# Seven half-depth products for the last four weight blocks of a first fp32 layer

## The chip, the cores and the metric

One core of one Trainium2 chip. The metric is device time of one execution in microseconds (us), the median of several runs.

## The reference

A retention layer (a decayed linear attention; 2 batches, 8 heads, 768 positions, head size 64) feeds two feed-forward layers, each with its own weights and curve. All arithmetic is in fp32; the weights and q, k, v are drawn at random.

```python
state = gamma * state + k_t (x) v_t          # for each batch and head
y_t   = q_t @ state / sqrt(64)
x = y as [1536 tokens, 512]                  # n_tokens = 2 * 768
h = x @ w_in;  g = softplus(h);    x = g @ w_out        # layer one, d_ff = 2048
h = x @ w_in2; g = s * relu(h)**2 + b;  out = g @ w_out2   # layer two
```

## The kernel before

**Number format.** TensorE multiplies in fp32r. Every fp32 operand is split into a high part (a copy rounded to fp32r, made by ScalarE) and a low part (operand minus high part, made by GpSimd or VectorE), and a product is three matmuls: high x high, high x low, low x high. The names end in `h` and `l`: `xh`/`xl` (the layer's input), `gh`/`gl` (the curve's output), `wh`/`wl` (weights).

**Tiles.** Tokens form three tiles (`j` = 0, 1, 2) of 512. Each layer has 16 blocks of 128 hidden units; the blocks are numbered 0 to 15 in layer one and 16 to 31 in layer two. For a block and a tile, the *first product* (12 matmuls of 128x128 by 128x512, one PSUM bank) gives h; the curve and the split give `gh`, `gl`; the *second product* (12 matmuls, `acc_mm` or `acc_2`) adds to four PSUM banks (`acc`) which hold one tile's 512 output columns. After some blocks those four banks are added to `xa[j]` in SBUF (`take_out`, `take_2`) and are used for the next tile. There is one set of these four banks. Beside them there are the banks `h`, `y`, `third` for first products and `word` for the weights' bits.

**Two ways of going through a layer.** In *steps* (`steps`, `step`), four blocks go through the three tiles, one block and one tile at a time: 12 steps for a group of four blocks, each with one first product (`h_mm`, 12 matmuls) and the second product of three steps earlier. In *pairs*, two blocks are taken together. `plain` makes all of their first products as 12 matmuls each (`all_of`), six of them. `second` uses seven half-depth products (`six`, 6 matmuls each, Strassen's scheme in Winograd's form) for tiles 0 and 1 of the two blocks, where plain products would take eight times six; tile 2 is done plainly in layer one. Each product of `second` is followed by a second product of earlier blocks. The seven products need four sums of weights (`sums_w`: four 128x256 sums on GpSimd; `split_sums`: their high parts on ScalarE, low parts on GpSimd) and four sums of x (`sum_x`, `parts_x`: t1 to t4), and their results are joined by copies on ScalarE (`kept`: p1, p5, u2) and adds on VectorE (`joined`).

**Order of layer one before.** Blocks 0 to 3 in steps, blocks 4 and 5 plain, blocks 6 to 11 as three pairs by `second(0, 3)` to `second(0, 5)`, and blocks 12 to 15 in twelve steps again. `take_out` after those steps adds the sums to `xa` on VectorE and splits the result into `xh` (ScalarE) and `xl` (GpSimd) for tiles 0 and 1; for tile 2, `sum_last` and `parts_last` do it, reading from PSUM. Layer two starts with `plain(1, 0)` (blocks 16 and 17), whose loop index k = 0 to 5 is called plain product 0 to 5 here, in the order tile 0 block 16, tile 0 block 17, tile 1 block 16 and so on. Then come `second(1, 1)` (blocks 18 and 19; during it the sums `sum_z` are made on VectorE for a finer scheme of tile 2 in the later pairs) and `second(1, 2)` to `second(1, 7)`.

**Weights.** They come as 64-bit words and are made into fp32 by `split_w`, in four pieces spread over the products by `part`, `go_first`, `go_last`, `end_part` and `go`: two VectorE operations (L291, L293) with a ScalarE copy (L296) into a buffer `wm` of which there are two, a VectorE operation (L301), and the split (ScalarE, GpSimd). The list `halves` gives their order, and also when `sums_w` (written `(w, 2)`) and `split_sums` (`(w, 3)`) run. The copy L296 of a weight must wait until all that read its `wm` buffer are done, `sums_w` among them.

**What sets the order.** Nothing is scheduled by a planner: each engine works through its own queue in the order in which the program issues to it, and waits in order. Within a product of `plain` in layer two the issue order is: the product, the curve (three ScalarE operations: relu L567, square L592, scale L593), the split of g (ScalarE, GpSimd), the pieces of weights left over, the second product, further weight pieces, `sum_x`, `parts_x`.

Of the kernel before, what the change touches and what calls it, by code (L numbers as in the profile page):

```python
# [13 lines left out]
P = 128  # L14
# [13 lines left out]
NG = NF // FG  # L28
# [14 lines left out]
P0, P1 = FG // 2, PAIRS - FG // 2  # L43
# [6 lines left out]
def tile_retention_mlps(ctx: ExitStack, tc: tile.TileContext, head, w1, w2, sb, out):  # L50
# [282 lines left out]

    steps = [(0, g, j, f4) for g in range(NG) for j in range(NTILE) for f4 in range(FG)]

# [46 lines left out]
    def act_3(s):  # L382
        gg_t[s] = next_g() if s >= GS else [gp.tile([P, TT], F32R, tag=t, name=t) for t in ("gh", "gl")]
# [24 lines left out]
    def take_out(s, cc):  # L408
        la, g, j, f4 = steps[s]
        ps, dst = acc_t[la, g, j][cc], xa[j][:, cc, :]  # L410
        if g == 0:
            nc.scalar.activation(dst, ps, AF.Copy)
        else:
            nc.vector.tensor_tensor(out=dst, in0=ps, in1=dst, op=ALU.add)
        if g == NG - 1:
            split(xh[j][:, cc, :], xl[j][:, cc, :], dst, nc.scalar, nc.gpsimd)


    def sum_last(banks):

        la, g, j, _ = steps[NS - 1]
        for cc in banks:
            t = acc_t[la, g, j][cc]
            nc.vector.tensor_tensor(out=t, in0=t, in1=xa[j][:, cc], op=ALU.add)

    def parts_last():
        la, g, j, _ = steps[NS - 1]
        ps = acc_t[la, g, j]
        for cc in range(KC):
            nc.scalar.activation(xh[j][:, cc], ps[cc], AF.Copy)  # L430
        for cc in range(KC):
            nc.vector.tensor_tensor(out=xl[j][:, cc], in0=ps[cc], in1=xh[j][:, cc].bitcast(F32), op=ALU.subtract)
# [228 lines left out]
    for p in range(P0, P1):  # L661
        halves += pair(0, p)
    at[0, P1] = len(halves)
    for w in (2 * P1, 2 * P1 + 2):
        halves += [(w, 0), (w + 1, 0)]
    halves += [(w, 1) for w in range(2 * P1, NF)]
# [96 lines left out]
    with tc.manual_schedule():  # L763
# [198 lines left out]
        def plain(la, p, left, sums, parts):  # L962
# [5 lines left out]
            for k, (j, half) in enumerate((j, half) for j in range(NTILE) for half in range(2)):  # L968
# [3 lines left out]
                if la and k == 2:  # L972
                    end_part()
                    accs[k]()
# [7 lines left out]
                if not la or k != 2:  # L982
                    accs[k]()
# [6 lines left out]
        def second(la, p):  # L990
# [3 lines left out]
            halved = la and p >= HALVED  # L994
            base -= halved
# [83 lines left out]
            if before:  # L1079
                parts_z(2)  # L1080

# [7 lines left out]
            for banks in (FIRST, SECOND) if la and p == PAIRS - 1 else (FIRST + SECOND,):  # L1089
                acc_2(la, p, 0, 1, banks)  # L1090
                take_2(la, p, 0, banks)
            finish(la, p, 1, 2, hb)
            go_last()
            if before:
# [61 lines left out]
        for p in range(P0 + 1, P1):  # L1156
            second(0, p)
        end_part()
        S1 = NS - GS
        for s in range(S1, NS):  # L1160
            k = s - S1
            if k < 4:
                accs = [of_pair(0, P1 - 1, 1 + k // 2, k % 2)]
            else:
                accs = [of_step(s - LAG)] if k > 4 else [of_step(S1), of_step(S1 + 1)]
            lim = at[1, 1] if k < GS - 1 else at[1, 1] + 1
            step(s, accs, 0 if k > 4 and ends(s - LAG) else lim, lo=nc.gpsimd if k < 5 else None)
            if k == GS - 1:
                sums_1 = all_x()
                next(sums_1)  # L1170
        act_3(NS - 1)
        act_hi(NS - 1)
        act_lo(NS - 1)

        def end():
            for banks in (FIRST, SECOND):
                acc_mm(NS - 1, banks)
                sum_last(banks)
            parts_last()

        left = [lambda s=s: acc_mm(s, FIRST + SECOND) for s in range(NS - LAG, NS - 1)] + [end]
        plain(1, 0, left, [[sums_1], [sums_1], [], [sums_1], [], []], [(1,), (3, 2), (), (4,), (), ()])
# [100 lines left out]
```

## Time and profile before

| | us |
|---|---|
| median of 3 runs | 563.57 (563.29 to 563.73) |
| the profiled execution, its own time | 563.33 |
| its span in the trace, first to last instruction | 561.4 |
| busy: TensorE / VectorE / ScalarE / GpSimd | 556.8 / 385.1 / 347.7 / 347.1 |

The profiled execution's time holds 1.93 us that lie outside the span. In the rows below, PE is TensorE's matmuls, DVE is VectorE, ACT is ScalarE, POOL is GpSimd; a row of a timeline gives start and duration, then line, operation, output and input tiles, and in brackets the idle time before it with what ended it.

### The profile page before, as it was taken

To read this page: it belongs to the slowest core of one execution; us is meant where nothing else is said; L and a number is where in the kernel's file an instruction comes from. 1 tells how busy PE (TensorE), PEld (TensorE's weight loads), DVE (VectorE), ACT (ScalarE), POOL (GpSimd) and SP (SyncE) were. 2 spreads that over 40 slices of the span, in tenths; PEclk is the share of its full clock that TensorE was granted. 3 is DMA by queue.
4 is the path that set the end of the run, shared out by engine and by line. 5 is a ranking of instruction groups with operands and counts; after the bars stand their busy time and mean duration, and the time that the engine had idled before them with its cause. 6 is when DMAs were issued, how large, how long until landed. Compare 5 with 4: busy or idle time off the path is not lost.

```text
span 561.4 us, 8357 instructions
## 1 busy us (share of the span) xinstructions
PE 556.8 (99%) x3080; PEld 464.6 (83%) x3080; DVE 385.1 (69%) x584; ACT 347.7 (62%) x638; POOL 347.1 (62%) x293
## 2 busy tenths in 40 slices
PE   8999999999999999999999999999999999999997
PEld 7877888888888888888888888888888888888886
DVE  4887768776767759776868879955655655656334
ACT  4766663544555655543427797958597786868561
POOL 4457467776598797833515996947466655646230
PEclk9999999999999999999999999999999999999999
DMA  8996111101222213322111031212221121110005
GB/s 343 406 360 224 41 39 62 51 15 62 75 76 64 87 37 92 115 95 75 57 57 52 24 110 61 92 39 76 75 76 45 69 75 49 65 38 2 0 13 213
DMA packets 15016, 50.61 MB, mean 90 GB/s; under 512 B 1792, under 2 KB 2048, under 8 KB 14976
## 3 DMA queue, kind: packets, MB, share of 16 engines
q1 hardware_dynamic: 14976, 50.08, 25.4%
q8 instruction: 24, 0.39, 0.3%
q14 instruction: 16, 0.13, 0.1%
HBM read 46.93 MB, written 3.15 MB: 89 GB/s over the span
## 4 chain that ended last, share of the span: by engine, by line
PE 98%; DVE 1%; ACT 0%; issue 0%; DVEq 0%
PE acc L621 35%; PE acc L404 12%; PE h L494 10%; PE h L353 8%; PE y L494 8%; PE third L494 5%; PE y L502 4%; PE third L502 4%; PE y L353 4%; PE y L192 2%; PE h L502 2%; PE s L173 2%; PE h L192 1%; PE acc L784 1%; PE acc L173 1%; PE acc L192 1%
## 5 line engine op out<-in xcount | busy, mean ns | idle before, releaser
L116 POOL TENSOR_TENSOR wl<-wm,wh 128x512 fp32r<-128x512 f32 x64 | 84.0, 1313 | 101.1 <-ACT wh L113 99.2
L116 POOL TENSOR_TENSOR gl<-c,gh 128x512 fp32r<-128x512 f32 x69 | 92.1, 1342 | 68.7 <-ACT gh L113 46.9
L631 DVE TENSOR_TENSOR xa<-acc,xa 128x512 f32<-128x512 f32 x131 | 82.3, 684 | 71.9 <-PE acc L621 71.7
L621 PE MATMUL acc<-wh,gl 128*128 128x512 f32 x190 | 74.3, 391 | 0.0
L621 PE MATMUL acc<-wh,gh 128*128 128x512 f32 x190 | 74.2, 390 | 0.0
L621 PE MATMUL acc<-wl,gh 128*128 128x512 f32 x190 | 53.6, 390 | 0.0
L113 ACT ACTIVATE gh<-c 128x512 fp32r<-128x512 f32 x69 | 43.6, 632 | 10.9 <-POOL c L595 6.9
L296 ACT ACTIVATE wm<-raw 128x512 f32<-128x512 f32 x64 | 42.4, 662 | 7.1 <-POOL wl L116 7.0
L301 DVE SCALAR_TENSOR_TENSOR wm<-wm,cu,word 128x512 uint32<-128x512 uint32 x54 | 40.0, 740 | 4.5 <-ACT wm L296 3.8
L113 ACT ACTIVATE wh<-wm 128x512 fp32r<-128x512 f32 x64 | 39.7, 620 | 4.2 <-DVE wm L301 4.1
L293 DVE SCALAR_TENSOR_TENSOR word<-raw,cu,word 128x512 uint32<-128x512 uint32 x54 | 40.8, 756 | 1.9
L621 PEld LDWEIGHTS acc<-wl,gh 128*128 128x128 f32 x190 | 35.7, 188 | 7.6
L621 PEld LDWEIGHTS acc<-wh,gh 128*128 128x128 f32 x190 | 35.8, 188 | 6.8 <-issue 0.4
L621 PEld LDWEIGHTS acc<-wh,gl 128*128 128x128 f32 x190 | 35.8, 188 | 6.7
L593 ACT ACTIVATE c<-c,sbt 128x512 f32<-128x512 f32 x48 | 39.2, 817 | 1.6
L366 ACT ACTIVATE t<-t 128x512 f32<-128x512 f32 x24 | 15.1, 628 | 39.0 <-DVE t L360 39.0
L404 PE MATMUL acc<-gh,wh 128*128 128x512 f32 x96 | 38.0, 395 | 0.0
L404 PE MATMUL acc<-gl,wh 128*128 128x512 f32 x96 | 37.4, 390 | 0.0
L291 DVE TENSOR_SCALAR word<-raw 128x512 uint32<-128x512 uint32 x54 | 37.1, 687 | 0.5
L621 PE MATMUL acc<-gh,wh 128*128 128x512 f32 x96 | 37.3, 389 | 0.0
L621 PE MATMUL acc<-gl,wh 128*128 128x512 f32 x96 | 37.3, 389 | 0.0
L567 ACT ACTIVATE c<-c 128x512 f32<-128x512 f32 x21 | 13.1, 633 | 36.8 <-DVE c L560 36.8
(274 smaller groups left out, 1453.3 us busy)
## 6 DMA issues: line engine op xcount, KB each, us to landing
raw<-w SPq DMA_DIRECT2D x64, 512.0 KB, 3.6
qk<-head SPq DMA_DIRECT2D x12, 512.0 KB, 8.3
kv<-head SPq DMA_DIRECT2D x12, 512.0 KB, 8.5
out<-xa SPq DMA_DIRECT2D x11, 256.0 KB, 2.1
cst<-head SPq DMA_DIRECT2D x1, 518.0 KB, 4.4
cst<-head SPq DMA_DIRECT2D x1, 256.0 KB, 5.4
out<-xa SPq DMA_DIRECT2D x2, 128.0 KB, 1.8
sbt<-sb SPq DMA_DIRECT2D x1, 1.0 KB, 10.4
```

The costliest lines, as they stand in the source:

```text
L113: nc.scalar.activation(hi, src, AF.Copy)
L116: lo_eng.tensor_tensor(out=lo, in0=src, in1=hi.bitcast(F32), op=ALU.subtract)
L293: nc.vector.scalar_tensor_tensor(out=x, in0=hw, scalar=cu[:, 0:1], in1=x, op0=ALU.bitwise_and, op1=ALU.bitwise_or)
L296: nc.scalar.activation(m, hw.bitcast(F32), AF.Copy, scale=REBIAS)
L301: nc.vector.scalar_tensor_tensor(out=m.bitcast(U32), in0=m.bitcast(U32), scalar=cu[:, 1:2], in1=x, op0=ALU.logical_shift_left, op1=ALU.bit ...
L353: nc.tensor.matmul(ps, w[:, cc * P : (cc + 1) * P], r[j][:, cc, :], start=i == 0, stop=i == len(ops) - 1)
L404: nc.tensor.matmul(acc_t[la, g, j][cc], *ops[i], start=f4 == 0 and i == 0, stop=ends(s) and i == 2)
L494: nc.tensor.matmul(ps, w[a][:, k * P : (k + 1) * P], x[b][:, k], start=start and i == 0, stop=i == len(ops) - 1, skip_group_check=True,)
L502: nc.tensor.matmul(ps, w[a][:, k * P : (k + 1) * P], (xh, xl)[b][j][:, k], start=i == 0, stop=i == len(ops) - 1)
L593: nc.scalar.activation(c, c, AF.Identity, scale=sbt[:, 0:1], bias=sbt[:, 1:2])
L621: nc.tensor.matmul(acc_t[la, p, "pair", j][cc], *ops[i], start=half == 0 and i == 0, stop=half == 1 and i == 2)
L631: nc.vector.tensor_tensor(out=dst, in0=ps, in1=dst, op=ALU.add)
```

## The change

Layer one's last four blocks (12 to 15) no longer go in twelve steps but as two more pairs by `second(0, 6)` and `second(0, 7)`, with the sums of weights that this needs. In the last pair (`final`), the second products of a tile's two blocks stand together: tile 0 after its own block 14 is finished, then tile 1's two, and tile 2's two move into `plain(1, 0)`. The new `x_whole` makes `xh` on ScalarE and `xl` on VectorE (before: GpSimd) for tiles 0 and 1 from `xa`; `x_last` does for tile 2 what `sum_last` and `parts_last` did. In `plain(1, 0)` two second products of layer one are left instead of three, one of the six places for a second product is empty, the special order of plain product 2 is gone, and the four sums of x come one behind each of plain products 0 to 3, with their parts one product later.

```diff
...
-P0, P1 = FG // 2, PAIRS - FG // 2
+P0 = FG // 2
...
-    steps = [(0, g, j, f4) for g in range(NG) for j in range(NTILE) for f4 in range(FG)]
+    steps = [(0, 0, j, f4) for j in range(NTILE) for f4 in range(FG)]
...
-        if g == 0:
-            nc.scalar.activation(dst, ps, AF.Copy)
-        else:
-            nc.vector.tensor_tensor(out=dst, in0=ps, in1=dst, op=ALU.add)
-        if g == NG - 1:
-            split(xh[j][:, cc, :], xl[j][:, cc, :], dst, nc.scalar, nc.gpsimd)
...
+        nc.scalar.activation(dst, ps, AF.Copy)
+
+
+    def x_whole(j):
+        for cc in range(KC):
+            nc.scalar.activation(xh[j][:, cc], xa[j][:, cc], AF.Copy)
+        for cc in range(KC):
+            nc.vector.tensor_tensor(
+                out=xl[j][:, cc], in0=xa[j][:, cc], in1=xh[j][:, cc].bitcast(F32), op=ALU.subtract
+            )
+
+    def x_last(j):
+        ps = acc_t[0, PAIRS - 1, "pair", j]
+        for cc in range(KC):
+            nc.vector.tensor_tensor(out=ps[cc], in0=ps[cc], in1=xa[j][:, cc], op=ALU.add)
         for cc in range(KC):
             nc.scalar.activation(xh[j][:, cc], ps[cc], AF.Copy)
...
-    for p in range(P0, P1):
+    for p in range(P0, PAIRS):
         halves += pair(0, p)
-    at[0, P1] = len(halves)
-    for w in (2 * P1, 2 * P1 + 2):
-        halves += [(w, 0), (w + 1, 0)]
-    halves += [(w, 1) for w in range(2 * P1, NF)]
+    at[0, PAIRS] = len(halves)
...
-                if la and k == 2:
-                    end_part()
-                    accs[k]()
...
-                if not la or k != 2:
-                    accs[k]()
+                accs[k]()
...
+            final = not la and p == PAIRS - 1
...
+            if final:
+                whole(*of_pair(la, p, 0, 1))
+                x_whole(0)
...
-            for banks in (FIRST, SECOND) if la and p == PAIRS - 1 else (FIRST + SECOND,):
-                acc_2(la, p, 0, 1, banks)
-                take_2(la, p, 0, banks)
+            whole(*of_pair(la, p, *((1, 0) if final else (0, 1))))
             finish(la, p, 1, 2, hb)
             go_last()
+            if final:
+                whole(*of_pair(la, p, 1, 1))
+                x_whole(1)
...
-        for p in range(P0 + 1, P1):
+        for p in range(P0 + 1, PAIRS):
             second(0, p)
-        end_part()
-        S1 = NS - GS
-        for s in range(S1, NS):
...
-            if k == GS - 1:
-                sums_1 = all_x()
-                next(sums_1)
...
         def end():
-            for banks in (FIRST, SECOND):
-                acc_mm(NS - 1, banks)
-                sum_last(banks)
-            parts_last()
-
-        left = [lambda s=s: acc_mm(s, FIRST + SECOND) for s in range(NS - LAG, NS - 1)] + [end]
-        plain(1, 0, left, [[sums_1], [sums_1], [], [sums_1], [], []], [(1,), (3, 2), (), (4,), (), ()])
+            acc_2(0, PAIRS - 1, 2, 1)
+            x_last(2)
+
+        sums_1 = all_x()
+        left = [lambda: acc_2(0, PAIRS - 1, 2, 0), end, lambda: None]
+        plain(1, 0, left, [[sums_1], [sums_1], [sums_1], [sums_1], [], []], [(), (1,), (3,), (2,), (4,), ()])
```

## Rows read from the trace of the kernel before

**Rows 1.** The page's head, TensorE's busy time and its granted clock.

```profile
span 561.4 us, 8357 instructions
PE 556.8 (99%) x3080; PEld 464.6 (83%) x3080; DVE 385.1 (69%) x584; ACT 347.7 (62%) x638; POOL 347.1 (62%) x293
PEclk9999999999999999999999999999999999999999
```

**Rows 2.** Chain of waits in order of time: start, length, what (twelve matmuls a piece).

```profile
231.70 2.72 PE h L353 x12
...
275.22 2.96 PE acc L404 x12
...
297.25 2.96 PE acc L404 x12
...
319.28 2.99 PE acc L621 x12
...
330.43 1.36 PE h L494 x6
...
335.87 1.36 PE y L494 x6
...
346.75 1.36 PE h L494 x6
```

**Rows 3.** Busy time by stretch: PE, PEld, DVE, ACT, POOL, clock, DMA.

```profile
200.42:231.70 31.28, 31.28 (x139) 25.90 (x139) 25.23 (x39) 18.63 (x33) 25.16 (x22) 1.00 0.26 85
302.96:330.43 27.47, 27.47 (x122) 22.45 (x121) 20.81 (x26) 23.43 (x37) 24.44 (x19) 1.00 0.14 47
330.43:361.71 31.28, 31.28 (x139) 25.90 (x139) 28.70 (x37) 25.42 (x43) 25.85 (x22) 1.00 0.25 85
```

**Rows 4.** Timeline of VectorE: low parts, bank takes, sums of x and z.

```profile
231.28 2.48 DVE L631 TENSOR_TENSOR xa<-acc,xa 128x512 f32<-128x512 f32 x4 [0.83 <-PE acc L621]
...
266.97 1.72 DVE L390 TENSOR_TENSOR gl<-t,gh 128x512 fp32r<-128x512 f32 x1
...
288.46 0.68 DVE L390 TENSOR_TENSOR gl<-t,gh 128x512 fp32r<-128x512 f32 x1
...
310.83 2.14 DVE L448 TENSOR_TENSOR xa<-xa,xa 128x1024 f32<-128x1024 f32 x1
...
338.95 2.54 DVE L545 TENSOR_TENSOR p<-p,xl 128x512 f32<-128x512 f32 x2
341.42 2.47 DVE L629 COPY xa<-acc 128x512 f32<-128x512 f32 x4
```

**Rows 5.** Timeline of GpSimd in the same stretch.

```profile
266.85 1.29 POOL L116 TENSOR_TENSOR wl<-wm,wh 128x512 fp32r<-128x512 f32 x1 [5.41 <-ACT wh L113]
...
305.91 1.30 POOL L116 TENSOR_TENSOR gl<-c,gh 128x512 fp32r<-128x512 f32 x1 [4.26 <-issue]
...
311.85 2.27 POOL L116 TENSOR_TENSOR gl<-c,gh 128x512 fp32r<-128x512 f32 x1
...
315.34 0.73 POOL L320 TENSOR_TENSOR ws<-wm 128x256 f32<-128x256 f32 x1
...
320.74 2.56 POOL L488 TENSOR_TENSOR x2l<-xa,x2h 128x512 fp32r<-128x512 f32 x2
...
328.00 2.55 POOL L116 TENSOR_TENSOR sl<-ws,sh 128x512 fp32r<-128x512 f32 x2
```

**Rows 6.** Timeline of ScalarE, plain products 0 to 5 and the pair behind.

```profile
303.00 0.60 ACT L567 ACTIVATE c<-h 128x512 f32<-128x512 f32 x1 [0.74 <-PE h L502]
...
305.68 0.62 ACT L113 ACTIVATE wh<-wm 128x512 fp32r<-128x512 f32 x1
...
330.47 0.60 ACT L567 ACTIVATE c<-y 128x512 f32<-128x512 f32 x1
...
334.24 0.58 ACT L508 ACTIVATE p<-h 128x512 f32<-128x512 f32 x1
...
339.47 0.58 ACT L508 ACTIVATE p<-y 128x512 f32<-128x512 f32 x1
```

More of the change, by code (lines that the diff above doesn't have):

```diff
@@ L27 @@
 FG = 4
-NG = NF // FG
 RING = 6
@@ L382, in act_3 @@
     def act_3(s):
-        gg_t[s] = next_g() if s >= GS else [gp.tile([P, TT], F32R, tag=t, name=t) for t in ("gh", "gl")]
+        gg_t[s] = [gp.tile([P, TT], F32R, tag=t, name=t) for t in ("gh", "gl")]
     def act_hi(s):
@@ L410, in take_out @@
         ps, dst = acc_t[la, g, j][cc], xa[j][:, cc, :]
-        if g == 0:
-            nc.scalar.activation(dst, ps, AF.Copy)
-        else:
-            nc.vector.tensor_tensor(out=dst, in0=ps, in1=dst, op=ALU.add)
-        if g == NG - 1:
-            split(xh[j][:, cc, :], xl[j][:, cc, :], dst, nc.scalar, nc.gpsimd)
[L419 to L428, printed above, removed]
+        nc.scalar.activation(dst, ps, AF.Copy)
[10 more added lines that the diff above has]
+            nc.vector.tensor_tensor(out=ps[cc], in0=ps[cc], in1=xa[j][:, cc], op=ALU.add)
         for cc in range(KC):
@@ L1155, in tile_retention_mlps @@
         plain(0, P0, left, [[sums_0], [], [], [], [], []], [(), (3,), (), (), (), ()])
-        for p in range(P0 + 1, P1):
+        for p in range(P0 + 1, PAIRS):
             second(0, p)
-        end_part()
-        S1 = NS - GS
-        for s in range(S1, NS):
[L1161 to L1167, printed above, removed]
-            if k == GS - 1:
-                sums_1 = all_x()
-                next(sums_1)
-        act_3(NS - 1)
-        act_hi(NS - 1)
-        act_lo(NS - 1)
-        def end():
-            for banks in (FIRST, SECOND):
-                acc_mm(NS - 1, banks)
-                sum_last(banks)
-            parts_last()
-        left = [lambda s=s: acc_mm(s, FIRST + SECOND) for s in range(NS - LAG, NS - 1)] + [end]
-        plain(1, 0, left, [[sums_1], [sums_1], [], [sums_1], [], []], [(1,), (3, 2), (), (4,), (), ()])
+        def end():
+            acc_2(0, PAIRS - 1, 2, 1)
[3 more added lines that the diff above has]
+        plain(1, 0, left, [[sums_1], [sums_1], [sums_1], [sums_1], [], []], [(), (1,), (3,), (2,), (4,), ()])
         for p in range(1, PAIRS):
```

## The prediction, made before the change was run

> **What bounds the kernel now.** [...] Next the chain of waits in order of time: from 231.70 on it names nothing but TensorE, and a piece of twelve matmuls takes 2.72 us there, 226.7 ns a matmul [rows 2]. Three pieces of the stretch that the change touches are longer: 2.96, 2.96 and 2.99 [rows 2]. The first matmul of each new tile's second product found its bank still being read (the two at the end of a group by `take_out`, the last by `parts_last`). That is 0.24 + 0.24 + 0.27 = 0.75 us. Then the busy time by stretch: in the plain pair that opens layer two GpSimd has 24.44 us of work in 27.47, and begins only 2.95 us into it (305.91 against 302.96); in the pair after it VectorE has 28.70 in 31.28 [rows 3, 5]. The helpers have little left just where the change takes TensorE time away.
>
> **What is saved.** Two pairs of `second` need 2 x (7 x 6 + 2 x 12) = 132 matmuls for first products where twelve steps need 12 x 12 = 144; second products stay at 144. So 12 matmuls go: 12 x 226.7 ns = 2.72 us. The three long pieces go too: in the new order a tile's banks have 2.72 us or more of other products between the last and the first second product, as in the pairs of rows 2, where no piece is long, and `x_last` has two products' time (5.44 us) instead of one. Saved: 2.72 + 0.75 = 3.47 us.
>
> **What is added and hidden.** The two pairs add sums of weights, copies and joins, and 12 adds to `xa`. A pair of this kind is in the trace: 31.28 us for 138 matmuls, exactly their spacing, with 25.23 us on VectorE, 18.63 on ScalarE and 25.16 on GpSimd [rows 3]. `second(0, 6)` and `second(0, 7)` issue the same, so I cost them at nothing; if the cover were gone, GpSimd's 25.16 would have to grow by 6. The weight DMAs on SP's queue are the same in number, three deep, in another order of halves, and cost nothing either.
>
> **The end of layer one.** `x_whole` puts four ScalarE copies and four VectorE subtracts behind tile 0's takes. A low part on VectorE takes 0.68 us when GpSimd is quiet, and 1.72 when a GpSimd operation of 1.29 began 0.12 earlier: it ended 0.55 after that operation did [rows 4, 5]. Four subtracts thus cost 2.4 to 6.9 us. I take the lower end, since GpSimd's next work there waits for ScalarE, which is at `x_whole`'s copies. Tile 0's last second product ends 8.16 us (three pieces) before plain product 0 reads `xl`; takes end 2.1 us after such an end (231.28 + 2.48 against 231.70 [rows 2, 4]), so even 6.9 nearly fits: cost 0, at most 0.5. [...]
>
> **The opening of layer two.** Let t = 0 be the end of plain product 0 (302.96 before [rows 3]). Before, ten pieces of 2.72 lay between it and the end of plain product 5; now nine do, since one place for a second product is empty. `second(1, 1)` starts at t = 24.48, not 27.47 [rows 2, 3]. Against that the helpers get more: one high and one low part of layer one's last block, one more weight split (the weights run one place later than before), and the same four sums of x. I walk through the queues in issue order with the rows' spacing.
>
> *ScalarE.* Relu, square, scale and high part take 2.68 us (303.00 to 305.68 [rows 6]). ScalarE was busy for 23.43 us in this stretch; with two more copies of 0.62 it has 24.7, or 25.0 with the issue gaps: already as long as the stretch. It also waits: 1.1 us for product 1; 1.4 us for the two x3 sums on VectorE, which take turns with GpSimd's low parts; 1.9 us at weight (18, 1), whose copy needs the `wm` buffer that the four `ws` sums on GpSimd still read. So its relu of product 5 comes at 0.04 + 25.0 + 4.4 = 29.4, which is 4.9 us after the product; before it was 0.04 after (330.47 against 330.43 [rows 2, 6]).
>
> *GpSimd.* To the first low part of the weights' sums (`sl`) of blocks 18 and 19 there are 17 operations of 1.25 (2.56 for two, 1.29 for one [rows 5]) and four `ws` of 0.7: 21.25 + 2.8 = 24.05, against 14 and 4 before. They begin at 2.95, wait 2.3 us for ScalarE (x1's high part stands behind `x_last`'s copies), and lose 4.4 us to VectorE's sums of x (the sum of 2.14 us held GpSimd's operation beside it up by 2.27 - 1.25 = 1.0 [rows 4, 5]; 1.1 for each of four). `sl` lands at 2.95 + 24.05 + 2.3 + 4.4 = 33.7. Before, it landed at 328.00 + 1.27 = 329.3.
>
> *What TensorE then meets.* Its second product in `second(1, 1)` (p5, at 335.87 before, 5.44 after the start [rows 2]) reads `sl` from the fifth matmul on: due at 24.48 + 5.44 + 0.91 = 30.83. Before, the slack was 336.78 - 329.3 = 7.5 us; now it is -2.9. A first stall, with 0.3 of it at the banks, as the takes of tile 0 stand behind the delayed sum of x on VectorE: **0.3 + 2.7 = 3.0 us**.
>
> *VectorE behind ScalarE.* In `second(1, 1)` VectorE's last weight operation waits for ScalarE's copy after product 5, at 29.4 + 2.7 + 0.7 = 32.9; then the join with p1, three operations of the next weight, the first z sum, two weight operations, two more z sums and the takes. The two z sums took 2.54 before, 1.2 more than alone, with GpSimd partly idle [rows 4]; now GpSimd has a queue, and each waits for one operation of it, some 3 us for the three. The takes run from 42.6 to 45.1; before they began at 341.42, or 10.99 after the pair's start, now 18.1 after [rows 2, 4]. TensorE, 3.0 late, waits 0.3 for the copy of p5 (ScalarE needs 5.23 from p1 to p5 [rows 6]) and is at the next tile's second product at 41.4; its four banks come free from 43.3 to 45.1, while it would need the last at 42.7: **2.4 us**. The bank `h`, free after one weight operation and two joins (47.0), is wanted for the product that stood 16.32 after the start (346.75 [rows 2]), and costs **0.5** more. Together 3.0 + 0.3 + 2.4 + 0.5 = 6.2 us. From there VectorE has fewer weights ahead, and the lag is gone by the next pair; TensorE runs without gaps to the end, so what it lost stays lost.
>
> **The sum.** 563.33 (the profiled execution: 561.4 of span and 1.93 outside) - 3.47 + 6.2 = 566.1. The median of the runs is 0.24 above that execution: 566.3. For these waits no row shows the whole thing, so the bounds: nothing if the slack of 7.5 us covers all, 6.2 + 1.7 if each of the three helper queues is half a microsecond or so slower than walked. I take the walk, since GpSimd's count, 24.05 us of operations due by 30.83 that cannot begin before 2.95, leaves 3.8 us for all waits, and the rows already show single ones of 1.0 to 1.2.
>
> **Rivals.**
> - *The helpers keep up (faster).* Place: `sl` and the relu of product 5. Price: none, so 563.57 - 3.47 = 560.1. It decides if GpSimd loses under 3.8 us to waits and VectorE's sums, and ScalarE's relu comes within 2.9 us of its product. For it: before, both had slack of 2.4 us and more (p1's copy ended at 334.82, its bank was wanted at 337.2). Against it: the count above, and ScalarE's 25.0 us for a stretch of 24.48.
> - *Only GpSimd is late (no change).* The stall at `sl` comes, but ScalarE and VectorE catch up while TensorE waits: 563.57 - 3.47 + 3.0 = 563.1. For it: ScalarE waits for others in 4.4 of its 29.4 us, and waits can shrink. Against it: a stall at `sl` does not bring VectorE's takes forward, which hang on ScalarE's copy after product 5.
> - *The wait moves to the end of layer one.* If `x_whole`'s subtracts alternate with GpSimd, tile 1's takes come late for tile 2's second product: 0.5 us on top of any case. That the seven products don't run without gaps is against the three pairs before [rows 3].
>
> **How the numbers follow.** Forecast, slower: 0.50, with a range of its own of 564.7 to 568.0. Only GpSimd late, 562.4 to 564.7: 0.20. Keeping up, 560.0 to 562.4: 0.30. A measurement of this kernel tells 0.2% (1.1 us) from no change. Since both signs hold much of the chance, the range takes in all but a tenth: 560.0 to 568.0.
>
> **What would show it.** Right: about 12 matmuls fewer on the page; pieces of 2.72 through `second(0, 6)`, `second(0, 7)` and plain products 0 to 5 with none of 2.96; then, in the pair behind, gaps at y <- x1, sh (the first over 2 us, ended by GpSimd's `sl`) and at the second product that follows the takes L629, with relu L567 of product 5 several us after its product. Wrong: if that relu follows its product within 3 us and `sl` lands before the fifth matmul of p5, the pair is dense and the time is near 560; if long pieces show at the tile changes of the last pair of layer one, the end of layer one is the place that I costed at nothing.

## The result, and the profile after

| | us |
|---|---|
| kernel before, median of 6 runs | 563.48 (563.21 to 563.73) |
| changed kernel, median of 6 runs | 568.70 (568.51 to 570.70) |
| ratio | 1.0098 (1.0084 to 1.0112) |

The change makes the kernel 5.2 us slower. The forecast was 2.7 us slower (6.2 - 3.47), with 568.0 as the upper end of the range. The ratios in this document are taken over all runs, so they are not the quotients of the medians. The profiled execution of the changed kernel took 570.70: 2.27 us of it were lost ahead of the edited stretch, whose first piece starts at 233.97 (below) and started at 231.70 [rows 2]; all of that lies in the first 25.3 us, and by their times (568.51 to 568.97) the other five executions didn't have it. So stretches and intervals are compared here, not points in absolute time. The mean granted clock was 1.000 in the executions of 570.70 and 568.51 and 0.997 in the other four; 570.70 - 2.27 is 568.43, so by these times the clock accounts for about half a microsecond of the 5.2 at most.

The page's head, TensorE's row and its clock, after:

```profile
span 568.8 us, 8388 instructions
PE 557.6 (98%) x3068; PEld 464.3 (82%) x3068; DVE 386.3 (68%) x590; ACT 360.7 (63%) x660; POOL 374.8 (66%) x317
PEclk9999999999999999999999999999999999999999
```

Beside [rows 1]: 3068 matmuls for 3080, the twelve fewer that were counted. The chain of waits (start, length, what) in layer one's two new pairs and the start of layer two:

```profile
233.97 1.36 PE h L490 x6
...
292.67 2.79 PE acc L617 x11
295.46 2.72 PE y L498 x12
298.18 5.44 PE acc L617 x24
303.62 2.72 PE h L498 x12
306.34 2.72 PE acc L617 x12
...
322.05 1.59 POOL gl L115
...
330.46 2.27 POOL x3l L484
...
334.00 1.44 POOL x2l L484 x2
```

The 2.96 and 2.99 of [rows 2] are gone: the saving of 3.47 us is there. The piece at 292.67 has only eleven matmuls: the twelfth stands ahead of a wait, which is shown below. And from 322 on the chain is GpSimd's until 340.2 (a wait there is shown below), which in [rows 2] it never was. Busy time by stretch (PE, PEld, DVE, ACT, POOL, clock, DMA): `second(0, 6)`, then from the end of plain product 0 to the end of plain product 5, then the pair behind, `second(1, 1)`:

```profile
233.97:265.25 31.28, 31.28 (x140) 25.90 (x139) 21.78 (x34) 17.88 (x31) 25.81 (x23) 1.00 0.20 68
306.34:331.01 24.67, 24.67 (x109) 20.20 (x109) 20.19 (x25) 20.39 (x34) 18.78 (x15) 1.00 0.17 53
331.01:368.45 37.44, 32.50 (x139) 25.59 (x139) 30.21 (x39) 27.69 (x47) 31.90 (x25) 1.00 0.20 64
```

`second(0, 6)` runs as densely as the pair in [rows 3], and but for 0.2 us so does the shortened plain stretch (nine pieces are 24.48 us). In that stretch ScalarE and GpSimd did 3.0 and 5.7 us less than in [rows 3], and in the pair behind 2.3 and 6.1 us more: their work slid into that pair, where TensorE is busy for 32.50 of 37.44 us.

TensorE's timeline, the rows that begin after a wait (in brackets: the idle time and what ended it):

```profile
291.32 0.49 PE L617 MATMUL acc<-gh,wh 128*128 128x512 f32 x1 [0.23 <-ACT gh L112]
292.67 0.50 PE L617 MATMUL acc<-gl,wh 128*128 128x512 f32 x1 [0.86 <-POOL gl L115]
...
340.25 0.73 PE L490 MATMUL y<-x1h,sl 128*128 128x512 f32 x2 [2.90 <-POOL sl L115]
...
349.19 0.50 PE L617 MATMUL acc<-wh,gh 128*128 128x512 f32 x1 [1.39 <-DVE xa L625]
...
365.63 0.50 PE L617 MATMUL acc<-wh,gl 128*128 128x512 f32 x1 [0.62 <-POOL gl L115]
...
379.69 0.50 PE L490 MATMUL y<-xh,sh 128*128 128x512 f32 x1 [0.37 <-ACT p L504]
```

What a wait costs is read here from the starts of the matmuls, as what lies above the spacing of 226.7 ns; that is some 0.25 us more than the bracket (3.18 for 2.90, 0.63 for 0.37). In this way the places cost 1.62 (291.3 to 293.0), 0.16 (311.9, a row not shown), 3.18, 1.67, 0.30 (352.2, not shown), 0.88 and 0.63 us, 8.44 in all. 8.44 - 3.47 = 4.97, of 5.22 measured.

The helpers' timelines behind these waits. VectorE (compare [rows 4]):

```profile
297.44 2.49 DVE L417 TENSOR_TENSOR xl<-xa,xh 128x512 fp32r<-128x512 f32 x4
...
311.56 1.36 DVE L444 TENSOR_TENSOR xa<-xa,xa 128x1024 f32<-128x1024 f32 x1
...
338.67 0.75 DVE L300 SCALAR_TENSOR_TENSOR wm<-wm,cu,word 128x512 uint32<-128x512 uint32 x1 [3.30 <-ACT wm L295]
...
344.58 3.36 DVE L541 TENSOR_TENSOR p<-p,xl 128x512 f32<-128x512 f32 x2
347.86 2.47 DVE L625 COPY xa<-acc 128x512 f32<-128x512 f32 x4
```

GpSimd (compare [rows 5]; the first row is from `second(0, 6)`):

```profile
260.07 1.29 POOL L115 TENSOR_TENSOR gl<-u,gh 128x512 fp32r<-128x512 f32 x1 [0.74 <-ACT gh L112]
...
291.34 1.28 POOL L115 TENSOR_TENSOR gl<-u,gh 128x512 fp32r<-128x512 f32 x1 [0.74 <-ACT gh L112]
...
311.80 2.28 POOL L115 TENSOR_TENSOR wl<-wm,wh 128x512 fp32r<-128x512 f32 x1
...
338.93 2.53 POOL L115 TENSOR_TENSOR sl<-ws,sh 128x512 fp32r<-128x512 f32 x2
```

ScalarE (compare [rows 6]):

```profile
328.58 0.66 ACT L295 ACTIVATE wm<-raw 128x512 f32<-128x512 f32 x1 [1.06 <-POOL ws L319]
...
335.28 0.57 ACT L563 ACTIVATE c<-y 128x512 f32<-128x512 f32 x1
...
361.06 0.67 ACT L295 ACTIVATE wm<-raw 128x512 f32<-128x512 f32 x1 [2.61 <-POOL ws L319]
...
374.06 0.60 ACT L504 ACTIVATE p<-h 128x512 f32<-128x512 f32 x1 [1.57 <-POOL xl L115]
```

Product 5 ended at 331.01; its relu starts at 335.28, 4.3 us later. Before, it was 0.04.

### The profile page after: what moved, and what is told of

It reads as the page before. It is cut to its first block, busy times and chain, and to the rows that moved or that the text cites. A ratio compares the mean times of both kernels' runs of the same rounds, so it can differ in the third digit from the quotient of the medians.

```text
span 568.8 us, 8388 instructions
## 1 busy us (share of the span) xinstructions
PE 557.6 (98%) x3068; PEld 464.3 (82%) x3068; DVE 386.3 (68%) x590; ACT 360.7 (63%) x660; POOL 374.8 (66%) x317
## 4 chain that ended last, share of the span: by engine, by line
PE 84%; POOL 6%; ACT 4%; DVE 3%; issue 1%; DMA 1%; DVEq 0%; ACTq 0%; POOLq 0%
PE acc L617 34%; PE h L490 10%; PE y L490 8%; PE acc L403 6%; PE h L352 5%; PE third L490 5%; PE y L498 4%; PE third L498 3%; PE y L191 2%; POOL gl L115 2%; PE s L172 2%; PE h L498 1%; PE h L191 1%; POOL wl L115 1%; PE y L352 1%
## 5 line engine op out<-in xcount | busy, mean ns | idle before, releaser
L115 POOL TENSOR_TENSOR gl<-c,gh 128x512 fp32r<-128x512 f32 x79 | 104.0, 1322 | 73.3 <-ACT gh L112 53.7
L627 DVE TENSOR_TENSOR xa<-acc,xa 128x512 f32<-128x512 f32 x151 | 94.5, 684 | 76.0 <-PE acc L617 75.8
L115 POOL TENSOR_TENSOR wl<-wm,wh 128x512 fp32r<-128x512 f32 x64 | 85.5, 1336 | 84.3 <-ACT wh L112 84.1
L617 PE MATMUL acc<-gl,wh 128*128 128x512 f32 x144 | 56.2, 391 | 0.9 <-POOL gl L115 0.9
L112 ACT ACTIVATE gh<-c 128x512 fp32r<-128x512 f32 x79 | 49.8, 632 | 11.0 <-POOL c L591 7.0
L617 PE MATMUL acc<-gh,wh 128*128 128x512 f32 x144 | 56.1, 390 | 0.2 <-ACT gh L112 0.2
L617 PE MATMUL acc<-gh,wl 128*128 128x512 f32 x144 | 38.5, 389 | 0.0
L591 POOL TENSOR_TENSOR c<-c 128x512 f32<-128x512 f32 x25 | 33.5, 1346 | 2.1 <-ACT c L583 2.0
L617 PEld LDWEIGHTS acc<-gl,wh 128*128 128x128 f32 x144 | 27.0, 188 | 7.1 <-POOL gl L115 1.5
```

The lines of the kernel that those rows point to most:

```text
L112: nc.scalar.activation(hi, src, AF.Copy)
L115: lo_eng.tensor_tensor(out=lo, in0=src, in1=hi.bitcast(F32), op=ALU.subtract)
L617: nc.tensor.matmul(acc_t[la, p, "pair", j][cc], *ops[i], start=half == 0 and i == 0, stop=half == 1 and i == 2)
```

## The experiments

Line numbers are those of the changed kernel, with small shifts where lines were added. "Lost" and "loss" are counted as above; a "wait" is the idle time in the brackets. Each diff is cut to the lines that matter and is against the changed kernel unless it says otherwise. The last column names the theory, of those written down before the run, whose time held.

| kernel | median us | ratio to before (interval) | time held |
|---|---|---|---|
| e1: last product split | 567.78 | 1.0085 (1.0068 to 1.0102) | A |
| e5: low parts on GpSimd | 570.49 | 1.0125 (1.0105 to 1.0145) | A |
| e4: x sums as before | 572.65 | 1.0164 (1.0149 to 1.0179) | C |
| e2: third sum's parts late | 570.11 | 1.0117 (1.0100 to 1.0134) | none, slower |
| c1: ten pieces | 572.32 | 1.0160 (1.0143 to 1.0178) | none, slower |
| a1: no low parts of x sums | 568.08 | 1.0091 (1.0075 to 1.0108) | none, slower |
| a2: no scale | 567.11 | 1.0064 (1.0049 to 1.0079) | none, 0.6 above A |
| a3: neither | 566.03 | 1.0044 (1.0029 to 1.0059) | B |
| e3: one weight ahead | 568.63 | 1.0102 (1.0079 to 1.0125) | B |
| e6: e1 and e3 | 568.11 | 1.0079 (1.0062 to 1.0096) | A, within 0.1 |
| c2: c1, e1 and e3 | 569.24 | 1.0099 (1.0082 to 1.0116) | none, slower |
| b1: e6, low parts 2 and 4 on VectorE | 567.39 | 1.0074 (1.0059 to 1.0090) | B |
| b2: e6, all four there | 569.19 | 1.0102 (1.0082 to 1.0119) | none, slower |
| d3: e6, low part 4 there | 566.20 | 1.0048 (1.0033 to 1.0062) | none, between |
| d1: e6, fourth sum's parts later | 567.67 | 1.0087 (1.0055 to 1.0120) | B |
| f1: d1, weight behind p5 | 565.31 | 1.0038 (1.0023 to 1.0052) | B |
| f2: e6, weight behind p5 | 568.83 | 1.0091 (1.0069 to 1.0112) | none, slower |
| d2: e6, no low parts of x sums | 562.28 | 0.9978 (0.9969 to 0.9987) | A |

### The end of layer one

**e1.** Half of the last first product goes ahead of tile 0's second product of block 15, which gets 1.36 us more for its operand.

```diff
...
+            part(base + 7)
+            other = bank(ps_y, "y")
             if final:
+                all_of(other, (bh, bl), 2, slice(0, 6))
                 whole(*of_pair(la, p, 0, 1))
                 x_whole(0)
...
+                all_of(other, (bh, bl), 2, slice(6, 12))
+            else:
+                all_of(other, (bh, bl), 2)
```

> The changed kernel with one edit: in the last pair of layer one, the first six matmuls of the last first product (tile 2, block 15) go ahead of tile 0's second product of block 15, the other six stay behind it. Nothing is left out. Theory A (the 1.6 us that TensorE stood still there came from the missing product between the curve of tile 0, block 15, and the second product that reads its low part): the 1.36 us of matmuls cover most of it, the gap at that second product falls from 1.5 us to about 0.2, and the time from 568.7 to 567.3 or so. Rival B (TensorE arrives earlier at layer two and only waits longer for GpSimd there): the gap goes, the gap at the product p5 of blocks 18 and 19 grows from 3.1 to 4.5, and the time stays at 568.7.

0.92 us faster by the medians, though the intervals overlap; the trace decides. The loss at that second product falls from 1.62 to 0.3; the next low part of g, at 0.16 in the changed kernel, now costs 0.6. The order of the two products was the cause. Most waits of layer two stay; the first of them now has this behind it (TensorE's timeline):

```profile
337.47 1.22 PE L490 MATMUL y<-x1h,sl 128*128 128x512 f32 x2 [2.93 <-POOL sl L115]
338.48 0.63 PE L490 MATMUL h<-x2h,sh 128*128 128x512 f32 x1
338.91 0.63 PE L490 MATMUL h<-x2l,sh 128*128 128x512 f32 x1
```

Matmuls start 0.43 us apart, twice the usual, until 343.5, and the wait at the takes is gone: TensorE came later, and the takes were done by then.

**e5.** `x_whole`'s low parts go back to GpSimd.

```diff
-            nc.vector.tensor_tensor(
+            nc.gpsimd.tensor_tensor(
```

> The changed kernel with one edit: the low parts of x for tiles 0 and 1 at the end of layer one are made on GpSimd, as before the change, instead of VectorE. Nothing is left out. Theory A (VectorE has room there, and GpSimd has 5.3 us free ahead of plain product 0): the low parts take 5.1 us in place of 2.5; the curves of the last two tiles wait behind them on GpSimd, and the time is 568.7 to 571. [...]

1.8 us slower by the medians, with intervals that overlap. In the trace the loss for `gl` at 311.9 (now at 310.8) grows from 0.16 to 1.1, and behind the `sl` wait (2.88) the matmuls start 0.43 us apart from 340.2 to 341.9. So moving these low parts to VectorE is not what made the changed kernel slower; the prediction had that right.

### The order of the x sums

**e4.** The sums and their parts as in the kernel before.

```diff
+        next(sums_1)
...
-        plain(1, 0, left, [[sums_1], [sums_1], [sums_1], [sums_1], [], []], [(), (1,), (3,), (2,), (4,), ()])
+        plain(1, 0, left, [[sums_1], [sums_1], [], [sums_1], [], []], [(1,), (3, 2), (), (4,), (), ()])
```

> The changed kernel with one edit: the sums of x and their parts go back to the places that they had before the change (the first sum ahead of the plain pair, two sums' parts behind plain product 1). Nothing is left out. Theory A (the spacing is not what costs; GpSimd's idle 2.1 us ahead of the first sum's low parts would be filled): 0.5 to 2 us less, 566.7 to 568.2. [...] Rival C (the spacing was needed, with the sums together TensorE waits longer): above 569.5.

4 us slower than the changed kernel. The loss at `sl` shrinks to about 0.8, and others take its place: 1.1 each at the copies of p1 and p5, and the two largest (TensorE's timeline):

```profile
322.25 0.50 PE L498 MATMUL third<-xh,wh 128*128 128x512 f32 x1 [1.50 <-ACT c L563]
...
333.88 0.50 PE L490 MATMUL third<-xh,wh 128*128 128x512 f32 x1 [1.77 <-ACT c L563]
```

With the sums early, ScalarE's relu is late for the bank `third`. The distance of one product between the sums was needed in the shortened order; it is not what costs.

**e2.** Only the parts are moved: the third sum's by two products, the fourth's by one.

```diff
-        plain(1, 0, left, [[sums_1], [sums_1], [sums_1], [sums_1], [], []], [(), (1,), (3,), (2,), (4,), ()])
+        plain(1, 0, left, [[sums_1], [sums_1], [sums_1], [sums_1], [], []], [(), (1,), (), (2,), (3,), (4,)])
```

> The changed kernel with one edit: in the plain pair of layer two the parts of x sum 3 are made two products later, behind the low parts of the weights' sums, and those of sum 4 one later. Nothing is left out. GpSimd then has two operations of 1.25 us less ahead of the weights' sums' low parts, which land 2.5 us earlier: the gap of 3.1 us at the product p5 falls to about 0.6. Theory A (two late chains run side by side; ScalarE's relu of plain product 5 and the VectorE takes behind it stay where they were, so TensorE waits there instead): the gap at the takes grows from 1.7 to about 4, and the time is 568.2 to 568.7. Rival B (GpSimd's queue alone is what is lost, and the other gaps follow from it): about 2.5 us less, 566.2.

`sl` comes in time but for 0.6 us; the copy of p1 on ScalarE is then 1.9 late, the takes still 1.9, and behind p1 the matmuls start 0.43 us apart from 339.1 to 341.7: 1.4 us slower.

**c1.** Tile 1's last second product moves behind plain product 0, so that ten pieces lie there again, and the adds of `x_last` come in two halves, ahead of the curve of plain product 2, as before the change.

```diff
-            if final:
-                whole(*of_pair(la, p, 1, 1))
-                x_whole(1)
...
-            acc_2(0, PAIRS - 1, 2, 1)
+            for banks in (FIRST, SECOND):
+                acc_2(0, PAIRS - 1, 2, 1, banks)
+                x_add(2, banks)
...
-        left = [lambda: acc_2(0, PAIRS - 1, 2, 0), end, lambda: None]
+        left = [one, lambda: acc_2(0, PAIRS - 1, 2, 0), end]
```

> The changed kernel with layer one's second product of tile 1, block 15, moved from the last pair to behind plain product 0 of layer two, so that the opening of layer two has ten pieces of 2.72 us again, as before the change, and not nine; the last second product and the adds to it come ahead of the curve of plain product 2, as before. Nothing is left out, the matmuls are the same. Theory A (what is lost is that the same helper work stands against one product less): the deadlines of blocks 18 and 19 move back by 2.7 us against the helpers' work, ScalarE's relu of product 5 comes within 2.5 us of it, 3 to 5 us return: 563.5 to 566. Rival B (the helpers' order, not the number of pieces, sets it): within 1 us of 568.6.

Slower by 3.6 us: the `sl` wait goes, but the plain pair's own second product needs the banks that `x_last` still reads, behind the sums of x on VectorE (TensorE's timeline):

```profile
322.47 0.80 PE L620 MATMUL acc<-wh,gh 128*128 128x512 f32 x1 [4.60 <-DVE xl L431]
```

The empty place is thus time that `x_last` needs in this order; filling it in this way was not free.

### Which helper is late

**a1** leaves out the eight GpSimd low parts of layer two's x sums (the products read the high part instead).

```diff
-        for c in range(2):
+        for c in range(0 if la else 2):
...
-        x_t[k] = hi, lo
+        x_t[k] = hi, hi if la else lo
```

> The changed kernel without the eight GpSimd operations that make the low parts of layer two's four sums of x (the high parts stand in for them, so the layer-two product is only approximate; all matmuls stay). It takes 10 us off GpSimd's queue in the stretch and nothing off TensorE. Theory A (GpSimd's queue, with what it holds up on ScalarE and VectorE, is the whole of what is lost from plain product 5 on): the gaps at p5, at the takes, at the end of that pair and at the start of the next, 6.6 us together, go to under 1; only the 1.6 us in the last pair of layer one stay: 562 to 563. Rival B (ScalarE has 25 us of its own work for 24.5 and is late without GpSimd): the gap at p5 goes, those at the takes and behind stay at 3 us or more: 565 to 567.

Ten us of work less on GpSimd, and 0.6 us gained. The `sl` wait is gone; three others stand there, and the two behind them stay (TensorE's timeline):

```profile
338.64 1.20 PE L490 MATMUL h<-x2h,sh 128*128 128x512 f32 x4 [1.02 <-ACT p L504]
...
343.85 0.50 PE L490 MATMUL y<-xh,sh 128*128 128x512 f32 x1 [0.81 <-ACT p L504]
...
348.19 0.50 PE L617 MATMUL acc<-wh,gh 128*128 128x512 f32 x1 [1.28 <-DVE xa L625]
...
364.63 0.50 PE L617 MATMUL acc<-wh,gl 128*128 128x512 f32 x1 [0.62 <-POOL gl L115]
...
378.68 0.50 PE L490 MATMUL y<-xh,sh 128*128 128x512 f32 x1 [0.37 <-ACT p L504]
```

ScalarE and VectorE were late without these operations of GpSimd too; TensorE's wait for GpSimd had hidden it. The last two rows are the waits at 365.6 and 379.7 of the changed kernel, as long as there.

**a2** leaves out the curve's scale on ScalarE in the plain pair.

```diff
+            if p:
-            nc.scalar.activation(c, c, AF.Identity, scale=sbt[:, 0:1], bias=sbt[:, 1:2])
+                nc.scalar.activation(c, c, AF.Identity, scale=sbt[:, 0:1], bias=sbt[:, 1:2])
```

> The changed kernel without the scale-and-bias operation of ScalarE (L593 before) in the plain pair of layer two, six operations of 0.82 us (the curve of blocks 16 and 17 lacks s and b; all matmuls stay). Theory A (ScalarE's queue and GpSimd's are late side by side): the relu of plain product 5 comes 3 to 4 us earlier, the gaps at the copy of p1, at the takes and behind go, the one at the weights' sums' low parts (3.1 us) stays: 565 to 566.5. Rival B (ScalarE alone sets what is lost, GpSimd's low parts would come earlier too): 562 to 564. [...]

The loss at the takes falls from 1.67 to 0.38, so it hung on ScalarE in part, as walked; the loss at `sl` stays, 3.19.

**a3** leaves out both.

> Both left out at once: the low parts of layer two's sums of x on GpSimd, as in a1, and ScalarE's scale-and-bias in the plain pair, as in a2. Theory A (two helper queues are late side by side, and taking work from one alone only shows the other): what is lost from plain product 5 on, 6.6 us, goes to under 1.5, the 1.6 us at the end of layer one stays: 562 to 563.5. Rival B (VectorE is late by itself): the gap at the takes stays over 1.4 us, 565 or more.

Still 2.5 us slower than before. `sl` and ScalarE are in time, and VectorE's takes are not (TensorE's timeline), for it still has the operations of two weights and the z sums ahead of them:

```profile
344.20 0.50 PE L618 MATMUL acc<-wh,gh 128*128 128x512 f32 x1 [1.30 <-DVE xa L626]
```

### The weights' order

**e3.** One weight more, (18, 0), is split in the last pair of layer one, so that in layer two all come one place earlier.

```diff
             if final:
+                part(base + 8)
+                end_part()
+                go_first(halved)
                 whole(*of_pair(la, p, 1, 1))
                 x_whole(1)
+                go_last()
```

> The changed kernel with one edit: one more weight (block 18's first) is split in the last pair of layer one, so that all weights of layer two's opening run one place earlier, as before the change. Nothing is left out. Theory A (the order of the weights, one place late against shorter products, is what makes ScalarE, GpSimd and VectorE late together): ScalarE no longer waits 1.1 us for GpSimd's sums of weights, the low parts of these sums land 2 to 4 us earlier, the gaps at the end of the pair of blocks 18 and 19 and at the start of the next (0.9 and 0.6 us) go, and 3.5 to 5 us come back: 564 to 565. Rival B (the helpers' work for the stretch is the same and only moves, it is the stretch that is too short by the one second product): at most 1.5 us, 567.2 or more.

No change in time, but another picture. The waits at `sl`, at the takes, at 365.6 and at 379.7 are gone. For `sl`, which comes ahead of every loss of TensorE in layer two here, that is the weights' place. The three later ones this run alone can't settle, since TensorE now loses 7.2 us ahead of them and the helpers could catch up meanwhile; d2 below bears on them. One wait stands for them (timeline, rows of GpSimd, ScalarE and TensorE in order of time):

```profile
335.91 2.53 POOL L484 TENSOR_TENSOR x4l<-xa,x4h 128x512 fp32r<-128x512 f32 x2
338.41 1.28 POOL L115 TENSOR_TENSOR gl<-c,gh 128x512 fp32r<-128x512 f32 x1
339.65 2.48 POOL L115 TENSOR_TENSOR wl<-wm,wh 128x512 fp32r<-128x512 f32 x2
...
340.94 0.66 ACT L295 ACTIVATE wm<-raw 128x512 f32<-128x512 f32 x1 [4.57 <-POOL wl L115]
...
344.17 0.79 PE L490 MATMUL y<-xh,sh 128*128 128x512 f32 x1 [4.60 <-ACT p L504]
```

ScalarE's copy into `wm` waits for a low part that stands behind `x4l` and `gl` on GpSimd; the copy of p5 stands behind it. With it the matmuls start 0.43 us apart until 349.3, which costs 2.4 us more.

**e6.** e1 and e3 together.

> Both single edits that each closed a named wait together: the last first product of layer one split around tile 0's second product (which cut the wait there from 1.62 to 0.3 us), and one more weight split ahead of layer two (which closed the waits at the takes, at 365.6 and at 379.7, but left one wait of 4.76 us at the product that needs p5's copy, with the matmuls at twice their spacing behind it). Theory A, the three helper queues are each about as long as the shortened opening, so edits add only where they don't hand work to the same queue: the split is worth its 0.9 us again, 567.5 to 568.0, with the wait at p5 as long as in that run. Theory B, the waits are independent of each other and each edit is worth its waits: 568.7 - 1.3 - 3.2 = 564.2 or less.

The loss at p5's copy is 5.0 us, and the split is worth 0.5 by the medians: of the 1.3 that it gives, a new loss of 0.62 at tile 1's banks (303.3) and 0.27 more at p5's copy take most back.

**c2.** c1 with e1 and e3.

> c1 with the split last product of e1 and the weights one place earlier of e3. Theory A: the parts add up, as each takes the lag at another place: the gap at tile 0's second product goes (1.3 us), the gaps at the p5 copy that stopped e3 go with the longer stretch: 560.5 to 563. Rival B (the helper queues are still late together behind plain product 5): 564 to 567.

Waits of 3.19 at `x_last` and 3.16 at p5's copy: filling the empty place doesn't help here either.

**b1, b2 and d3.** On e6, low parts of the x sums are taken from GpSimd to VectorE: of sums 2 and 4 (b1), of all (b2), of sum 4 (d3).

```diff
-            nc.gpsimd.tensor_tensor(out=lo[:, c], in0=src[c], in1=hi[:, c].bitcast(F32), op=ALU.subtract)
+            (nc.vector if la and k in (2, 4) else nc.gpsimd).tensor_tensor(out=lo[:, c], in0=src[c], in1=hi[:, c].bitcast(F32), op=ALU.subtract)
```

> The changed kernel with the split last product (e1), the weights one place earlier (e3), and the low parts of x sums 2 and 4 on VectorE instead of GpSimd. Nothing is left out. [...] Rival B (VectorE becomes late instead, its low parts wait for GpSimd's operations and hold up the takes): 564 to 568.

> As b1, but the low parts of all four sums of x in layer two on VectorE. Nothing is left out. Theory A (GpSimd's queue is the limit): GpSimd gets 10 us less work, no backlog is left, TensorE runs without gaps: 560 to 562. [...]

> The same two edits, with the two low parts of the fourth x sum alone on VectorE in place of GpSimd (with the second and the fourth there the time was 567.4 and VectorE was late). Theory A, the balance between the two queues decides, and two operations are what VectorE can take: GpSimd's queue ahead of the low part of weight (19, 1) is 2.5 us shorter and VectorE's is 1.4 to 2 us longer, the wait at p5 shrinks to 1 to 2.5 us, 563 to 566. Theory B, VectorE has no room for any more: a wait of over 3 us stays, now behind VectorE's operation, 567 or more.

b1 gains 0.7 on e6; now VectorE is what ScalarE waits for (timeline, rows of VectorE and ScalarE):

```profile
333.64 2.60 DVE L484 TENSOR_TENSOR x4l<-xa,x4h 128x512 fp32r<-128x512 f32 x2
...
339.13 0.63 ACT L563 ACTIVATE c<-c 128x512 f32<-128x512 f32 x1 [3.69 <-DVE c L556]
```

and TensorE waits 3.53 us for p5 in its turn. The busy time of the stretch behind that wait (PE, PEld, DVE, ACT, POOL, clock, DMA):

```profile
343.00:348.00 5.00, 4.60 (x13) 3.65 (x14) 4.76 (x6) 1.56 (x4) 4.71 (x5) 0.66 0.13 52
```

b2 has two waits, 3.94 at the takes and 1.97 at p5. d3 is the best of the three at 566.20, with 3.26 left at p5, between its two theories: by the medians VectorE has room for two operations, not for four.

**d1.** On e6, the fourth sum's parts one product later.

```diff
-        plain(1, 0, left, [[sums_1], [sums_1], [sums_1], [sums_1], [], []], [(), (1,), (3,), (2,), (4,), ()])
+        plain(1, 0, left, [[sums_1], [sums_1], [sums_1], [sums_1], [], []], [(), (1,), (3,), (2,), (), (4,)])
```

> The same two edits, and the two parts of the fourth x sum (two ScalarE copies, two GpSimd low parts) issued one product later. Theory A, ScalarE's copy into wm waits for GpSimd's queue ahead of the low part of weight (19, 1): two operations of 1.27 us fewer stand ahead of it, so the wait of 4.76 us at p5's copy shrinks by some 2.5 us, and the matmuls behind it keep their spacing more often: 563 to 565. Theory B, it is ScalarE's own length that makes p5's copy late: the two copies of 0.53 us are moved too, so the wait shrinks by 1.1 us or less and the time stays above 566.

The wait at p5's copy halves to 2.40 (4.87 in e6), by the 2.5 us of GpSimd work moved, as theory A has it. The runs spread from 565.68 to 572.13, at mean granted clocks of 1.000 to 0.991, the longest at the lowest: the median says little, the profiled execution took 565.86.

**f1 and f2.** In the pair behind, the first weight's steps are issued behind p5's copy; f1 on d1, f2 on e6.

```diff
             end_part()
-            go_first(halved)
+            behind = la and p == 1
+            if not behind:
+                go_first(halved)
...
-            go_last()
+            if not behind:
+                go_last()
...
             p5 = kept(other, "p5")
+            if behind:
+                go(late_work, 3)
```

> The kernel with the product split, the weight ahead and the fourth sum's parts one product later (565.7 to 572, with one wait of 2.55 us at p5's copy and matmuls at twice their spacing behind it), and in the pair after the plain one the three weight steps of the first product issued behind the copy of p5, so that ScalarE's copy of the weight, which waits for GpSimd, is no longer queued ahead of p5. Theory A, what is late is only what stands behind that one wait in ScalarE's queue: the 2.55 us and the wide spacing go, 561 to 562.5, below the kernel before. Theory B, ScalarE's queue is long by itself and p5's copy comes as late as before, or VectorE's operation on the same weight then holds the bank takes: a wait of over 1.5 us stays, 564 or more.

> The same move of the weight steps behind p5's copy, with the fourth sum's parts where the changed kernel has them (568.1 without the move, one wait of 5.7 us at p5's copy). Theory A, the wait is one of order in ScalarE's queue: it shrinks to below 1 us, 561.5 to 563.5. Theory B, GpSimd's backlog is real work that someone waits for in any order: the wait moves to the bank takes or to the next product's low parts and 2 to 4 us of it stay, 564 to 567.

(The wait of 5.7 us named in f2's text is e6's at p5's copy, 5.0 by the count used here.) p5's copy is in time within a microsecond in both, and the wait appears at the takes, 2.68 in f1 and 3.06 in f2, which also waits 1.64 for the copy of u2 (f1: timeline, rows of VectorE and TensorE):

```profile
339.29 0.75 DVE L300 SCALAR_TENSOR_TENSOR wm<-wm,cu,word 128x512 uint32<-128x512 uint32 x1 [1.83 <-ACT wm L295]
339.96 3.25 DVE L541 TENSOR_TENSOR p<-p,xl 128x512 f32<-128x512 f32 x2
...
344.46 0.50 PE L617 MATMUL acc<-wh,gh 128*128 128x512 f32 x1 [2.68 <-DVE xa L625]
```

So it isn't the order of one queue. f1 has the lowest median of the versions that compute everything, and is still 0.38% slower than the kernel before.

**d2.** On e6, the eight GpSimd low parts left out as in a1.

> The same two edits, with the eight GpSimd low parts of layer two's x sums left out (the product's operand is the high part in their place). Theory A, with the weights ahead only GpSimd's backlog is left: no wait over 0.5 us in the opening of layer two, 560.5 to 562.5. Theory B, ScalarE or VectorE is late by itself with the weights ahead too: a wait of over 1 us stays at p5's copy or at the takes, 564 or more.

Faster than the kernel before by 0.22%. One wait is left in the opening of layer two (TensorE's timeline):

```profile
339.55 0.50 PE L490 MATMUL y<-xh,sh 128*128 128x512 f32 x1 [0.56 <-ACT p L504]
```

The losses of this run in the two stretches are 0.30, 0.72 and 0.82 us; with them and the saving of 3.47, 563.52 becomes 561.9, and 562.28 was measured, so little is left that isn't accounted for. By a1 the same omission without the split and the weights ahead gave 0.6 us; with them it gives 5.8. It also bears on the three later waits that e3 left open: a1, with the low parts left out too, loses 1.55 at the takes, 0.88 at the end of the pair and 0.63 in the next, and here all three are gone although TensorE lost little before them. What differs is the weights' place and the split; the split alone (e1) left the last of them at 0.68, and the split with the low parts left out was not run. The amount of helper work and its place cost together, and either alone uncovers the other.

## Why the prediction was right or wrong

**The saving** was right: 12 matmuls and three long pieces, 3.47 us.

**The opening of layer two** was right in place, engine and order, and 1 us high. Counted from the end of plain product 0 (306.34 after), `sl` was put at 33.7 and landed at 33.9; the relu of product 5 at 29.4, it came at 28.9; the takes at 42.6, they began at 41.5. The stalls were 3.18 for 3.0 (with nothing of it at the banks), nothing for 0.3 at p5, 1.67 for 2.4, 0.30 for 0.5: 5.15 in place of 6.2. The rival in which only GpSimd is late falls: the takes waited too, and a1 and a3 show that the other two queues are late without GpSimd's low parts too.

**Failed: "cost 0, at most 0.5" for the end of layer one.** It cost 1.78 us. The step looked at the takes and the new low parts only, and those were in time: four in 2.49 us, the 2.4 that was taken. What it didn't look at is the order of products: with a tile's two second products together, tile 0's second one runs one product earlier, and its operand `gl` comes at the end of a long curve (relu, a VectorE operation behind four bank takes, softplus, a GpSimd add, the high part, the low part). That chain is no longer than in the pair ahead, where `gl` also starts 26.1 us into the pair (260.07 against 233.97, 291.34 against 265.25); it is needed sooner. e1 shows it. The third rival had the stretch, with another product, another mechanism and a third of the price. The upper case of the step was also added up wrong: 6.9 us exceed 8.16 - 2.1 by 0.8, not 0.5; it did not come up.

Beside a sum of x on VectorE that began at 311.56 and ended at 312.92, a GpSimd low part took 2.28 us from 311.80, where one takes 1.30 otherwise. At `x_whole` nothing of this kind cost TensorE time: its four low parts took 2.49 us, the pieces behind them have no wait (2.72, 5.44 and 2.72 from 295.46 on), and e5, with the low parts on GpSimd, was not faster.

**Failed: "the lag is gone by the next pair".** 0.88 us at the last second product of `second(1, 1)` and 0.63 in `second(1, 2)` came behind it. ScalarE waited there 2.61 us for GpSimd's `ws` sums and 1.57 for a low part. d2 beside a1 shows that the weights' place has its part in these (with e1 and e3 they go, without them they stay): the prediction named that the weights run one place later, counted one more split in the queues, and then let the delay end with the pair. But the lag went through that pair into the next; behind 380 the changed kernel loses no more than the kernel before.

With the two failed steps set right the sum would be 566.3 - 1.05 + 1.78 + 1.51 = 568.5. The range's upper end, 568.0, had bounds for the costed waits only; the two steps costed at nothing had one of 0.5 and none. The errors at the single places of the opening (0.2 low at `sl`, then 0.3, 0.7 and 0.2 high) are of the size that the prediction allowed its walk, half a microsecond or so a queue.

**Left open:** whether an order exists that keeps all of the work and is faster than the kernel before. None of those run was; what is shown is that moving work among the three helpers, or within one queue, moves the wait.

## What to carry to other kernels

When matmuls are cut from an engine that is 99% busy, the helpers' work per microsecond rises in that stretch; sum each helper's queue against the shortened stretch, and expect that relieving one queue shows the next. When an order is rearranged, check every operand of each product that moves forward, above all the end of the longest chain, and not only the operations that were edited. A queue that is late need not have caught up by the next stretch (here it had not), so price the stretches behind as well.

## What the runs showed of the hardware

TensorE's matmuls went to twice their spacing (0.43 us) behind some single waits: of 2.93 us in e1, 4.60 in e3, 3.53 in b1, where the granted clock of the stretch shown is 0.66, and 1.00 in the five microseconds ahead of it and behind it. Waits of 2.90 in the profiled execution of the changed kernel, 2.92 in a2 and 3.19 in c2 (the one at `x_last`) had no such spacing behind them, so the length of the wait alone did not decide; what does, no run here shows. In e3 the spacing cost 2.4 us on top of the wait; the prediction had no term for it.
